# r times the decays: one multiply for a pair of heads, then DMAs into the zeroed tile

## The chip, the cores and the metric

The kernel runs on one core of a Trainium2 chip. The metric is the device time of one execution in microseconds (us); before the change the median of 3 runs is 726.37 us (724.88 to 728.85). A core has five engines, each with its own queue of instructions that it works off in order: TensorE (PE, with its weight loads as PEld), VectorE (DVE), ScalarE (ACT), GpSimd (POOL) and SyncE (SP, which here only issues DMAs). A DMA is issued by one of these queues and then moved by 16 shared DMA engines.

## The reference, cut to what matters

Three stages follow each other for 4 batches. Stage A is a linear recurrence over time for 8 heads of width 48, with a decay `w` per step and channel; stage B is a mixture of four causal attention experts; stage C is a feed-forward block. The change touches stage A alone:

```python
for t in range(S):                       # S = 768
    cur = np.einsum('bhd,bhe->bhde', u[None] * kt, vt)
    y[:, :, t] = np.einsum('bhd,bhde->bhe', rt, state + cur)
    state = wt[:, :, :, None] * state + np.einsum('bhd,bhe->bhde', kt, vt)
```

## The kernel before

**Stage A in chunks.** Time is cut into 6 chunks of 128 steps and heads are taken in pairs, so there are 16 pairs over the 4 batches. Head h of a pair stands in partitions 64h to 64h + 47. Within a chunk the products of decays come from two scans on DVE: `suf` (line 220, from the chunk's end) and `ex` (line 246, from its start). k is multiplied by `suf` into `kt` (line 234), r by `ex` into `rt` (line 255). Both multiplies read the transposed input straight from PSUM (`ptr`, line 201), three chunks (a half) at a time.

**Why `rt` is written per head.** `rt` has, for each chunk, 128 columns for head 0 and 128 for head 1. It is zeroed once (line 165), and head h's rows are written only into head h's columns, so that one matmul with `kt` (line 329, `pg`) gives both heads' 128x128 score blocks without mixing them. So line 255 runs four times per pair, for two halves and two heads, each on 48 partitions and 384 columns. There are two `rt` tiles, used in turn.

**From `rt` on.** `pg` is copied by ACT into `at` (line 337) and masked by POOL (line 338); `y_unit` sums `at` times v, and `rt` times the carried state `um`, in PSUM (`py`, line 368); ACT and DVE split the result into two parts (`xs`, lines 382 and 383), which a DMA stores. The state comes from `pu` (line 298) through DVE (`um`, lines 307 and 313). ACT overwrites `suf` and `ex` with their absolute values (lines 270 and 271) for a range check, once line 234 and line 255 have read them.

**What sets the order.** The program is written as generators that are interleaved: `a_prep` of the next pair is woven into `a_pair` of the current one, beside the streams of stage B and of `c_convert` (line 810), which turns the weights of stage C into pairs of tiles, one block after another (`c_raw` by DMA, then `c_w` on ACT and DVE, `c_hi`, `c_lo`). Batch 0 of stage A runs with nothing but weight loading beside it (about the first 75 us), the other three with stage B and the conversion beside it (to about 314 us). Then stage A's memory is released, the weights of stage C are loaded, and stages B and C share the rest. On top of this a scheduler places the instructions on each engine by its own estimate of their times, so a change of a few instructions moves others around them too.

**SP's queue.** In stage A nearly all DMAs are issued by SP in one order: the inputs of the next pairs (lines 180 and 195: `nw`, `nk`, `nr`, `nv`), `xs` (lines 404 and 412), `c_raw` and the stores of the conversion (lines 797 and 817), the second copy of k (line 571) and the input of stage B (line 529). A DMA that waits for an engine holds back those behind it.

Of the kernel before, what the change touches and what calls it, by code (L numbers as in the profile page):

```python
# [8 lines left out]
F32 = mybir.dt.float32  # L9
# [6 lines left out]
OP = mybir.AluOpType  # L16
# [7 lines left out]
C = 128  # L24
NC_ = S // C
# [87 lines left out]
def rwkv_moe_kernel(ctx, tc, r, k, v, w, u, wg, wq, wk, wv, wo, mu_k, mu_r, w_k, w_v, w_r, out):  # L113
    nc = tc.nc
# [9 lines left out]
    pA = stageA.enter_context(tc.tile_pool(name="pA", bufs=1, side="right"))  # L124
# [10 lines left out]
    def ps_a(nm):  # L135
        tag = cyc["tags"][cyc["n"] % len(cyc["tags"])]
        cyc["n"] += 1
        return (psA if tag == "a" else ps).tile([128, 512], F32, tag=tag, name=nm, bufs=PSB[tag])
# [47 lines left out]
    def a_load(p, nm):  # L186
        if p >= B * NP:
            return
        b, pr = divmod(p, NP)
        if nm[0] == "n":  # L190
            loaded[p, nm] = load_nat(SRC[nm], b, pr)
        else:
            loaded[p, nm] = nats[nm]
            for h in range(2):
                nc.sync.dma_start(nats[nm][:, :, h, 0:D], SRC[nm][b, 2 * pr + h].rearrange("(c p) d -> p c d", p=C))

    def tr_in(nat, f):

        pt = ps_a("ptr")
        for x in range(3):  # L200
            nc.tensor.transpose(pt[:, x * C : (x + 1) * C], nat[:, 3 * f + x].rearrange("p h d -> p (h d)"), ident)
        return pt[:, 0:HALF].rearrange("p (c x) -> p c x", x=C)
# [6 lines left out]
    def a_prep(b, pr):  # L209
        p = b * NP + pr  # L210
        nw, nk, nr, vn = (loaded.pop((p, x)) for x in ("w", "k", "r", "nv"))
        j = 2 * p
        halves = [slice(3 * f, 3 * f + 3) for f in range(2)]
        chunks = lambda t, x, o=0: t[:, o : o + NC_ * x].rearrange("p (c x) -> p c x", x=x)[:, :, 0:C]
        for f, cs in enumerate(halves):
            nc.scalar.copy(chunks(X, XC, 1)[:, cs], tr_in(nw, f))
        a_load(p + 1, "w")
        yield 1
        suf = pA.tile([128, XW], F32, tag="suf", name="suf", bufs=SUFB)
        nc.vector.tensor_tensor_scan(  # L220
            out=suf[:, ::-1], data0=X[:, ::-1], data1=d1[:, ::-1], initial=0.0, op0=OP.mult, op1=OP.add
        )
        yield 1
        kt = pA.tile([128, S], F32, tag="kt", name="kt", bufs=2)

        ku = pA.tile([128, NC_, 2, D], F32, tag="ku", name="ku", bufs=1)
        nc.gpsimd.tensor_tensor(
            out=ku, in0=nk[:, :, :, 0:D], in1=ub[:, None, 2 * pr : 2 * pr + 2].to_broadcast([128, NC_, 2, D]), op=OP.mult
        )
        rt = rts[p % 2]  # L230
        sh = bass.AP(tensor=suf.tensor, offset=suf[:, 2:3].offset, ap=[suf[:, 2:3].ap[0], [XC, NC_], [1, C]])
        for f, cs in enumerate(halves):
            pk = tr_in(nk, f)
            nc.vector.tensor_tensor(out=chunks(kt, C)[:, cs], in0=pk, in1=sh[:, cs], op=OP.mult)
        a_load(p + 1, "k")
        yield 1

        pc = pA.tile([128, NC_], F32, tag="pc", name="pc", bufs=2)
        pcs = suf[:, 1 : 1 + NC_ * XC : XC]
        nc.vector.reciprocal(out=F1[:, 0 : NC_ * XC : XC], in_=pcs)  # L240
        nc.scalar.copy(pc, pcs)
        pcx = pcxs[p % 2]
        nc.gpsimd.tensor_copy(pcx[:, :, 1:], pc[:, None, 2:NC_].to_broadcast([128, D, NC_ - 2]))
        yield 1
        ex = pA.tile([128, NC_ * XC], F32, tag="ex", name="ex", bufs=1)
        nc.vector.tensor_tensor_scan(  # L246
            out=ex, data0=X[:, 0 : NC_ * XC], data1=F1[:, 0 : NC_ * XC], initial=0.0, op0=OP.mult, op1=OP.add
        )
        yield 1
        ev = chunks(ex, XC)  # L250
        for f, cs in enumerate(halves):
            pr_ = tr_in(nr, f)
            for h in range(2):
                q = slice(64 * h, 64 * h + D)
                nc.vector.tensor_tensor(out=rt[q, cs, h], in0=pr_[q], in1=ev[q, cs], op=OP.mult)  # L255
        nc.vector.tensor_tensor(out=ku, in0=ku, in1=nr[:, :, :, 0:D], op=OP.mult)
        a_load(p + 1, "r")
        cc = pA.tile([128, NC_, 2], F32, tag="cc", name="cc", bufs=2)
        nc.vector.tensor_reduce(out=cc, in_=ku, axis=AX.X, op=OP.add)
        dg = dgt[p % 2]  # L260
        nc.gpsimd.tensor_tensor(
            out=dg[:, :, :, 0:D].rearrange("p c h d -> p h c d"),
            in0=vn.rearrange("p (h c) d -> p h c d", h=2),
            in1=cc.rearrange("p c h -> p h c")[:, :, :, None].to_broadcast([128, 2, NC_, D]),
            op=OP.mult,
        )
        dgs[b, pr] = dg
        kts[b, pr] = kt
        yield 1
        nc.scalar.activation(out=suf, in_=suf, func=AF.Abs, accum_out=chk[:, j : j + 1])  # L270
        nc.scalar.activation(out=ex, in_=ex, func=AF.Abs, accum_out=chk[:, j + 1 : j + 2])
        yield 1
        prep[b, pr] = (rt, kt, vn, pc)
        yield 1
# [147 lines left out]
    def phase_a(b):  # L422
        if b == 0:
            for _ in a_prep(0, 0):
                pass
            a_kt(0, 0)
            yield 5 * 109
        for pr in range(NP):
            nxt = (b, pr + 1) if pr + 1 < NP else (b + 1, 0)
            if nxt[0] < B:  # L430
                yield from weave(a_pair(b, pr, nxt), a_prep(*nxt), 7, 8)
            else:
                yield from a_pair(b, pr, None)
            a_load(b * NP + pr + 2, "nv")
# [7 lines left out]
        out=cmask, in_=cmask, pattern=[[-1, 128]], compare_op=OP.is_ge, fill=NEG, base=0, channel_multiplier=1  # L442
# [782 lines left out]
```

## Time and profile before

| What | Value |
|---|---|
| median of 3 runs | 726.37 us (724.88 to 728.85) |
| profiled execution, its own time | 727.12 us |
| its span (first to last instruction) | 725.4 us |
| PE busy | 672.8 us (93%) |
| DVE busy | 497.9 us (69%) |
| ACT busy | 409.2 us (56%) |
| POOL busy | 299.7 us (41%) |
| mean granted PE clock | 0.984 |

The span is divided below at 75 us and at 314 us, where the chain of waits shows the end of batch 0 and of stage A. A busy share is an average over such stages; the chain of waits follows the work that ended last back through the engines and says which of them a stage waited for. All of the change lies ahead of 314 us.

### The profile page before, as it was taken

The numbers are of one execution on the slowest core, as the hardware profiler recorded it, in microseconds if no ns is written. First come the engines' busy times: TensorE is split into PE (matmuls) and PEld (weight loads), VectorE is DVE, ScalarE is ACT, GpSimd is POOL, SyncE is SP. The second block draws the span as 40 slices with busy tenths as digits, with TensorE's granted clock in tenths as the row PEclk, the third lists the DMA queues.
The fourth block names the chain that finished last, engine by engine and source line by source line (L and its number), as shares of the span: only waits on it lengthen the run. The fifth ranks groups of instructions, "written<-read, shape, count | busy, mean of one in ns | idle before, by whom it ended". The sixth has DMA issues, their size and how long they took to land.

```text
span 725.4 us, 13681 instructions
## 1 busy us (share of the span) xinstructions
PE 672.8 (93%) x4938; PEld 585.4 (81%) x4938; DVE 497.9 (69%) x938; ACT 409.2 (56%) x1117; POOL 299.7 (41%) x397
## 2 busy tenths in 40 slices
PE   5887978889799999997999999999999999999995
PEld 4776856676577786866999899889898888989995
DVE  8988899998999888754543756556457573729520
ACT  3554556666576566656735657465556656534530
POOL 5876444343445222204625435362343515352320
PEclk9999899999999999999999999999999999999999
DMA  8797666668677653159320103211101101220001
GB/s 157 152 184 173 176 180 175 170 174 251 148 198 186 170 126 83 33 187 411 100 67 11 45 12 99 98 34 44 55 34 44 23 13 34 86 68 23 12 23 38
DMA packets 144205, 77.88 MB, mean 107 GB/s; under 512 B 109824, under 2 KB 138752, under 8 KB 143616
## 3 DMA queue, kind: packets, MB, share of 16 engines
q1 hardware_dynamic: 139936, 64.73, 35.1%
q0 software_dynamic: 864, 7.47, 2.6%
q10 hardware_dynamic: 3328, 4.72, 1.8%
q8 instruction: 41, 0.67, 0.4%
q14 instruction: 36, 0.29, 0.1%
HBM read 47.40 MB, written 23.99 MB: 98 GB/s over the span
## 4 chain that ended last, share of the span: by engine, by line
PE 64%; DVE 18%; DMA 8%; issue 4%; ACT 3%; POOL 1%; SPq 1%; ACTq 0%; DVEq 0%; POOLq 0%
PE ph L871 14%; PE pvo L871 14%; PE pz L871 5%; PE pa L710 5%; PE pq L518 4%; PE pt L681 3%; PE po L518 3%; PE py L368 3%; PE pv L518 3%; DMA c_raw<-in_moe_w_v_dram 2%; DVE ex L246 2%; PE psc L624 2%; PE pg L329 2%; DVE suf L220 2%; DVE rt L255 2%
## 5 line engine op out<-in xcount | busy, mean ns | idle before, releaser
L633 DVE TENSOR_REDUCE st<-psc 128x1 f32<-128x384 f32 (+4 forms) x128 | 62.1, 499 | 56.4 <-PE psc L629 41.3
L891 POOL TENSOR_TENSOR rl<-rl 128x256 f32<-128x256 f32 (+1 forms) x88 | 59.3, 678 | 78.5 <-ACT rl L890 78.3
L865 POOL TENSOR_TENSOR ml<-m,mh 128x256 fp32r<-128x256 f32 x54 | 40.6, 751 | 108.5 <-ACT mh L864 97.4
L645 ACT ACTIVATE A<-psc,st 128x384 f32<-128x384 f32 (+4 forms) x128 | 68.8, 542 | 20.2 <-DVE st L642 13.3
L871 PE MATMUL ph<-mh,ckh 128*128 128x256 f32 (+1 forms) x264 | 78.8, 299 | 0.9 <-ACT m L858 0.8
L871 PE MATMUL ph<-mh,ckl 128*128 128x256 f32 (+1 forms) x264 | 76.9, 292 | 1.5 <-DMA ckl<-ck_l_scratch 1.5
L338 POOL TENSOR_SCALAR_AFFINE_SELECT at<-at 128x512 f32<-128x512 f32 x48 | 44.7, 932 | 79.2 <-ACT at L337 79.0
L871 PE MATMUL ph<-ml,ckh 128*128 128x256 f32 (+1 forms) x264 | 76.9, 294 | 0.0
L871 PE MATMUL pvo<-cvh,hh 128*128 128x384 f32 x192 | 65.5, 341 | 0.0
L329 PE MATMUL pg<-rt,kt 128*128 128x256 f32 x192 | 53.8, 407 | 12.3 <-DVE um L307 5.8
L894 POOL TENSOR_TENSOR hl<-rl,hh 128x256 fp32r<-128x256 f32 x72 | 53.8, 756 | 27.0 <-ACT hh L892 26.7
L871 PE MATMUL pvo<-cvl,hh 128*128 128x384 f32 x192 | 64.6, 336 | 0.0
L871 PE MATMUL pvo<-cvh,hl 128*128 128x384 f32 x192 | 64.0, 336 | 0.0
L681 PE MATMUL pt<-ident,A 128*128 128x128 f32 x336 | 57.7, 275 | 0.0
L624 PE MATMUL psc<-k,q 128*128 128x384 f32 (+4 forms) x128 | 49.0, 383 | 9.0 <-ACT A L645 6.2
L890 ACT ACTIVATE rl<-ph 128x256 f32<-128x256 f32 (+1 forms) x88 | 35.5, 405 | 37.6 <-PE ph L871 26.2
L871 PEld LDWEIGHTS ph<-mh,ckh 128*128 128x128 f32 x264 | 49.9, 189 | 3.3 <-ACT m L858 1.0
L710 PE MATMUL pa<-at,vs 128*64 128x384 f32 (+2 forms) x288 | 52.1, 425 | 0.5 <-ACT at L694 0.5
L871 PEld LDWEIGHTS ph<-mh,ckl 128*128 128x128 f32 x264 | 50.0, 190 | 1.8 <-DMA ckl<-ck_l_scratch 1.8
L871 PEld LDWEIGHTS ph<-ml,ckh 128*128 128x128 f32 x264 | 49.9, 190 | 1.5 <-issue 1.5
L329 PEld LDWEIGHTS pg<-rt,kt 128*128 128x128 f32 x192 | 34.4, 197 | 19.8 <-DVE um L307 6.8
L861 DVE SCALAR_TENSOR_TENSOR m<-x2c,mu,m 128x256 f32<-128x256 f32 (+1 forms) x66 | 35.2, 539 | 20.4 <-ACT m L858 15.8
(172 smaller groups left out, 1917.3 us busy)
## 6 DMA issues: line engine op xcount, KB each, us to landing
x_scratch<-xs SPq DMA_DIRECT2D x24, 288.0 KB, 4.0
x<-x_scratch SPq DMA_DIRECT2D x6, 1152.0 KB, 8.4
nw<-in_w_dram SPq DMA_DIRECT2D x32, 144.0 KB, 3.7
nk<-in_k_dram SPq DMA_DIRECT2D x32, 144.0 KB, 3.1
nr<-in_r_dram SPq DMA_DIRECT2D x32, 144.0 KB, 2.8
nv<-in_v_dram SPq DMA_DIRECT2D x16, 288.0 KB, 3.2
out_dram<-rg SPq DMA_DIRECT2D x24, 192.0 KB, 1.9
c_raw<-in_moe_w_k_dram SPq DMA_DIRECT2D x12, 256.0 KB, 3.3
```

Source lines behind the costliest of these rows:

```text
L329: nc.tensor.matmul(pg[:, x * 2 * C : (x + 1) * 2 * C], lhsT=kt[:, c * C : (c + 1) * C], rhs=rt[:, c].rearrange("p h x -> p (h x)"), start= ...
L338: nc.gpsimd.affine_select(out=av, in_=av, pattern=[[0, 4], [1, C]], compare_op=OP.is_gt, fill=0.0, base=0, channel_multiplier=-1)
L518: nc.tensor.matmul(out, lhsT=a, rhs=c, start=i == 0, stop=i == n - 1)
L624: nc.tensor.matmul(o, lhsT=qs[e][:, tsl], rhs=ks[e][:, s0:s1], start=True, stop=False, skip_group_check=True)
L633: nc.vector.tensor_reduce(out=st[:, si : si + 1], in_=o, axis=AX.X, op=OP.max, negate=True)
L645: nc.scalar.activation(out=A[:, s0:s1], in_=p[:, 0 : s1 - s0], func=AF.Exp, bias=nm, accum_out=st[:, 3 + si : 4 + si])
L681: nc.tensor.transpose(pt[:, (j - j0) * 128 : (j - j0 + 1) * 128], A[:, j * 128 : (j + 1) * 128], ident)
L710: nc.tensor.matmul(pa[64 * e : 64 * e + 64, t0:HALF], lhsT=vs[:, j, 2 * pr + e], rhs=at[e][:, c0 : c0 + HALF - t0], start=j == 0, stop=j = ...
L865: eng.tensor_tensor(out=lo[:, j], in0=m1, in1=hi[:, j].bitcast(F32), op=OP.subtract)
L871: nc.tensor.matmul(out, lhsT=a, rhs=c, start=i == 0, stop=i == n - 1)
L891: nc.gpsimd.tensor_tensor(out=rl_, in0=rl_, in1=rl_, op=OP.mult)
L894: eng.tensor_tensor(out=hl[:, m], in0=rl_, in1=hh[:, m].bitcast(F32), op=OP.subtract)
```

## The change

For each half, DVE now multiplies all 128 partitions at once into a new plain tile `rp` (one buffer), in which the rows of both heads share the same columns. Then SP issues two DMAs for each half, one for each head, that copy 48 partitions x 3 chunks x 128 columns into that head's columns of `rt`. `rt` stays zero elsewhere as before. PE now waits for DMAs where it waited for DVE.

```diff
         ev = chunks(ex, XC)
+
+        rp = pA.tile([128, NC_, C], F32, tag="rp", name="rp", bufs=1)
         for f, cs in enumerate(halves):
             pr_ = tr_in(nr, f)
+            nc.vector.tensor_tensor(out=rp[:, cs], in0=pr_, in1=ev[:, cs], op=OP.mult)
             for h in range(2):
                 q = slice(64 * h, 64 * h + D)
-                nc.vector.tensor_tensor(out=rt[q, cs, h], in0=pr_[q], in1=ev[q, cs], op=OP.mult)
+                nc.sync.dma_start(rt[q, cs, h], rp[q, cs])
         nc.vector.tensor_tensor(out=ku, in0=ku, in1=nr[:, :, :, 0:D], op=OP.mult)
```

Per pair this is 2 instructions on DVE in place of 4, and 4 more DMAs in SP's queue; over 16 pairs 32 in place of 64, and 64 more DMAs. The scheduler's order moves with it, within stage A only: behind the last pair every engine's order is the same as before.

PE, batch 0, around the first `pg` of the third pair (`rt_86`; `ptr` with `nw` and `nk` are the transposes of the fourth pair's w and k). Before:

```order
49 L329 MATMUL pg<-rt_86,kt 128x256 x2
50 L298 MATMUL pu<-nv_82,kh 64x48 x5
51 L201 MATMUL ptr<-ident,nw 128x128 x3
52 L298 MATMUL pu<-nv_82,kh 64x48 x5
53 L201 MATMUL ptr<-ident,nk 128x128 x3
54 L329 MATMUL pg<-rt_86,kt 128x256 x3
```

And now:

```order
51 L201 MATMUL ptr<-ident,nw 128x128 x3
52 L201 MATMUL ptr<-ident,nk 128x128 x6
53 L349 MATMUL py<-ident,dg_84 128x128 x3
54 L332 MATMUL pg<-rt_86,kt 128x256 x2
55 L301 MATMUL pu<-nv_82,kh 64x48 x10
56 L332 MATMUL pg<-rt_86,kt 128x256 x4
```

The next pair's transposes and three of this pair's own transposes into `py` now stand ahead of the first `pg`, which used to stand ahead of them.

DVE at the same place (third pair: `ex`, the products with r, then `xs` and `um`, and `suf` of the fourth). Before:

```order
33 L246 SCALAR_TENSOR_TENSOR ex<-wx,d1f 128x774
34 L255 TENSOR_TENSOR rt_86<-ptr,ex 48x3x128 x4
35 L383 TENSOR_TENSOR xs<-py,xs 128x384 x2
36 L307 TENSOR_TENSOR um<-pu,pc 128x240
37 L220 SCALAR_TENSOR_TENSOR suf<-wx,d_77 128x775
```

And now:

```order
32 L246 SCALAR_TENSOR_TENSOR ex<-wx,d1f 128x774
33 L262 TENSOR_REDUCE cc<-ku 128x12
34 L316 SCALAR_TENSOR_TENSOR um<-pcx_91,um 128x240
35 L255 TENSOR_TENSOR rp<-ptr,ex 128x384 x2
36 L386 TENSOR_TENSOR xs<-py,xs 128x384 x2
37 L220 SCALAR_TENSOR_TENSOR suf<-wx,d_77 128x775
```

Two instructions stand where four stood, and the third pair's `um` now comes later, behind the next `suf`.

SP in the middle of stage A, at the tenth pair, where stage B's input (`x`, 1152 KB each) is loaded. Before:

```order
133 L529 DMA x<-x_scratch 128x6x384
134 L571 DMA k_1767<-k_1767 64x384
135 L529 DMA x<-x_scratch 128x6x384
136 L797 DMA c_raw<-in_moe_w_v_dram 128x384 x2
137 L817 DMA cv_h_scratch<-c_hi 128x192
138 L817 DMA cv_l_scratch<-c_lo 128x192
139 L195 DMA nr<-in_r_dram 128x6x48 x2
```

And now:

```order
142 L532 DMA x<-x_scratch 128x6x384 x2
143 L800 DMA c_raw<-in_moe_w_v_dram 128x384
144 L258 DMA rt_87<-rp 48x3x128 x4
145 L195 DMA nr<-in_r_dram 128x6x48 x2
146 L820 DMA cr_h_scratch<-c_hi 128x192
```

The four new DMAs of this pair stand directly behind the two large loads.

## Rows read from the trace of the kernel before

**Rows 1.** The page: busy time, share of the span, instructions.
```profile
span 725.4 us, 13681 instructions
PE 672.8 (93%) x4938; PEld 585.4 (81%) x4938; DVE 497.9 (69%) x938; ACT 409.2 (56%) x1117; POOL 299.7 (41%) x397
```

**Rows 2.** Busy time by stage: columns as named in the first line.
```profile
core 0: us, PE busy (x) PEld busy (x) DVE busy (x) ACT busy (x) POOL busy (x), PEclk, DMA share, GB/s
0.00:75.00 75.00, 59.08 (x505) 47.78 (x506) 65.30 (x90) 36.00 (x86) 54.18 (x68) 0.93 0.81 169
75.00:314.00 239.00, 215.04 (x1821) 173.57 (x1819) 209.88 (x428) 149.02 (x411) 89.95 (x101) 0.98 0.61 155
340.00:725.00 385.00, 377.63 (x2483) 349.44 (x2481) 208.77 (x389) 208.70 (x576) 149.86 (x218) 1.00 0.16 50
```

**Rows 3.** Chain of waits by line, shares: 0 to 75 us, then 75 to 314.
```profile
by line: issue 16.4%; PE pg L329 7.9%; DVE rt L255 7.2%; PE py L368 6.6%; DMA ub<-in_u_dram 6.2%; PE ptr L201 5.8%; SPq L195 4.7%; POOL wvl L461 3.5%; POOL ku L227 3.5%; DMA nr<-in_r_dram 3.5%; DVE suf L220 3.1%; DVE um L313 3.1%; POOL at L
...
by line: DMA c_raw<-in_moe_w_v_dram 7.2%; DVE ex L246 6.4%; PE py L368 6.2%; issue 5.7%; DVE suf L220 5.0%; DVE st L633 4.2%; PE pg L329 4.0%; DMA k<-k 3.8%; DVE c_w L805 3.7%; DVE rt L255 3.3%; DVE kt L234 3.2%; PE pq L518 2.8%; DMA c_raw<
```

**Rows 4.** Instruction groups to 320 us: busy us, mean ns, idle before, releaser.
```profile
L255 DVE TENSOR_TENSOR rt<-ptr,ex 48x384 f32<-48x384 f32 x64 | 35.4, 553 | 3.5 <-PE ptr L201 2.2
...
L234 DVE TENSOR_TENSOR kt<-ptr,suf 128x384 f32<-128x384 f32 x32 | 16.6, 539 | 0.1
...
L271 ACT ACTIVATE ex<-ex 128x774 f32<-128x774 f32 x16 | 13.6, 852 | 13.6 <-DVE rt L255 13.5
```

**Rows 5.** Chain of waits in batch 0 and after: start, us, what.
```profile
39.14 0.57 DVE rt L255
39.72 0.02 issue
39.74 0.48 ACT ex L271
...
47.85 2.60 DMA nr<-in_r_dram
...
85.14 3.60 DMA c_raw<-in_moe_w_k_dram
...
167.79 9.46 DMA c_raw<-in_moe_w_v_dram
...
218.48 2.52 DMA c_raw<-in_moe_w_v_dram
```

**Rows 6.** Timeline: rt and first pg of pairs 3, 6, 15 (start, us).
```profile
37.42 2.28 DVE L255 TENSOR_TENSOR rt<-ptr,ex 48x384 f32<-48x384 f32 x4
38.81 0.73 PEld L329 LDWEIGHTS pg<-rt,kt 128*128 128x128 f32 x4
...
77.97 1.12 DVE L255 TENSOR_TENSOR rt<-ptr,ex 48x384 f32<-48x384 f32 x2 [0.57 <-PE ptr L201]
87.67 0.36 PEld L329 LDWEIGHTS pg<-rt,kt 128*128 128x128 f32 x2
...
276.57 2.27 DVE L255 TENSOR_TENSOR rt<-ptr,ex 48x384 f32<-48x384 f32 x4
281.39 0.73 PEld L329 LDWEIGHTS pg<-rt,kt 128*128 128x128 f32 x4
```

**Rows 7.** DMA issues (count, KB, us to landing); then one line's issue durations, ns.
```profile
x<-x_scratch SPq DMA_DIRECT2D x6, 1152.0 KB, 8.4
k<-k SPq DMA_DIRECT2D x32, 96.0 KB, 2.1
x<-xs SPq DMA_DIRECT2D x6, 288.0 KB, 4.6
...
L571 SPq DMA_DIRECT2D k<-k x32: 461/482/571, 96.5 to 577.9; - x32
```

**Rows 8.** SP's own waits from 75 to 300 us: total, times, longest.
```profile
SPq L797 <- DVE c_w L805: 28.4, 17, 5.3
SPq L180 <- PE py L368: 27.9, 8, 4.7
```

**Rows 9.** SP's timeline in batch 0: start, us.
```profile
29.02 1.23 SPq L195 DMA_DIRECT2D nw<-in_w_dram  x2
30.35 1.43 SPq L412 DMA_DIRECT2D x<-xs  x2
...
36.14 2.83 SPq L195 DMA_DIRECT2D nr<-in_r_dram  x2
39.08 0.56 SPq L469 DMA_DIRECT2D st<-in_moe_wk_dram  x1
39.73 0.46 SPq L180 DMA_DIRECT2D nv<-in_v_dram  x1
```

## The prediction, made before the result was known

> **What bounds the kernel now.** I read the page first for its busy times, then busy time by stage, then the chain of waits by line, and the timeline around the instructions that change. The page alone misleads: PE is busy for 672.8 of 725.4 us and DVE for 497.9 [rows 1], as if DVE had much to spare. By stage it is otherwise: DVE is busy for 65.3 of the first 75 us and for 209.9 of the next 239 (87% and 88%), PE for 59.1 and 215.0 (79% and 90%) [rows 2]. From 340 us on PE is busy for 377.6 of 385 us and bounds alone, and nothing that stands there changes place. So the question is how much earlier stage A ends, and stage A is bound by no single engine: DVE and PE hand the chain to each other, with DMAs between them. The reader is to see in the chain's shares that line 255 holds 7.2% of the first 75 us, 5.4 us, and 3.3% of the next 239, 7.9 us [rows 3]. That is 13.3 us on the path of the 35.4 us that line 255 costs DVE [rows 4]; the other 22 us lie beside something later.
>
> **DVE's part.** 64 products of 48 partitions take 553 ns each, 35.4 us. The new form, 128 partitions x 384 columns from PSUM, is the form of line 234, whose 32 take 539 ns each [rows 4]. So 48 rows cost as much as 128, and 32 new products cost 32 x 0.539 = 17.2 us. DVE is relieved of 18.2 us. On the chain half of each term goes: 2.7 us ahead of 75 us, 3.9 us behind it, 6.6 us together. In an unchanged order that is the most to be had to first order, since the chain moves to another engine when one link shortens. What comes behind line 255 on the chain is mostly not `pg` but ACT, which may not overwrite `ex` before the product has read it [rows 5]; ACT waits 13.5 us in all for this [rows 4], and that wait ends 1.1 us earlier for a pair where DVE alone sets it. What is late next is `at`, `xs` and `wx` behind it on ACT, and PE.
>
> **The DMAs' part.** The trace has no DMA of this shape. Each moves 48 x 3 pieces of 512 bytes, 72 KB. The nearest row is the copy of k from one SBUF half to the other, 96 KB, which lands 2.1 us after its issue and holds SP for 482 ns; the DMA of `xs` into `x`, also from SBUF to SBUF, with four times the bytes, lands after 4.6 us [rows 7]. Nothing excludes more than either where the queue is full: a `c_raw` load behind the large `x` loads took 9.46 us [rows 5]. I take 2.1 us, the nearer row, and keep 4.6 for the range. The first `pg` needs both heads of the first half, so it waits for the second of two DMAs: 0.48 us for the first issue, then 2.1 us, 2.6 us behind the first product.
>
> How much of it is covered is read from the timeline, from the end of the second product (the first half's second head) to the first `pg`. Pair 3, in batch 0: the products end at 37.42 + 2 x 0.57 = 38.56, `pg` starts at 38.81, 0.25 us later. Pair 6: 77.97 + 1.12 = 79.09 to 87.67, 8.6 us. Pair 15: 276.57 + 1.14 = 277.71 to 281.39, 3.7 us [rows 6]. These are the extremes of pairs 6 to 16, eleven of them; the middle one has 5.4. The new first product ends 0.57 us before the old second one, so the first `pg` could start 2.6 - 0.57, about 2.0 us, behind the old mark. From pair 6 on 3.7 us or more cover this, with at least 1.7 us left over. In batch 0 only 0.25 us do, and about 1.8 us per pair would be exposed in pairs 3 to 5. There the new order places nine transposes of the next pair and three of its own ahead of the first `pg`, which is work that PE had to do anyway. I let it cover 1.1 of the 1.8 us (between none and all), so 0.7 x 3 = 2.1 us come back, and 0.3 us for the start of pair 1, which has no earlier pair to hide behind: 2.4 us (between 0 and 3 x 1.8 + 2.0 = 7.4).
>
> **SP's part.** 64 issues of 0.48 us are 31 us more in SP's queue, four for each pair: 20 of them ahead of 75 us, 44 behind it. From 29.0 to 40.2 us SP issues almost without a gap [rows 9], so in batch 0 about 2 us for each pair come out of little room. Behind 75 us there is room, but an issue in the wrong place delays what stands behind it: seven times between 85.14 and 218.48 us the chain runs through the landing of a `c_raw` load [rows 5], because ACT and DVE, which work in order, wait for it. If two new issues stand ahead of such a load in one case of eight or so, that is 7 x 0.12 x 1, about 0.8 us. It could be nothing, where the scheduler places them behind, or 7 x 1.9 = 13 us, where all four stand ahead each time. I take 0.8 us, since SP already holds issues of the same length between those loads.
>
> The Trainium skill bears on this term from the other side: its page "DMA: Bandwidth & Descriptors", section "Issuing engines are not separate DMA queues", says that the sequencer's time to start a DMA is usually small beside the DMA itself. By that rule this term would be zero and the sum 0.8 us lower; here the rows show 0.48 of 2.1 us, almost a quarter, in a queue that was nearly full in batch 0, so I do not follow it.
>
> **The sum.** The profiled execution took 727.12 us, 1.7 us more than its span. 727.1 - 6.6 + 2.4 + 0.8 = 723.7. The median of the runs shown, 726.37, lies 0.75 us below the profiled execution, so the forecast for the median is **723.0 us**. Its own range, with the order's own shifts of some 3 us either way, is 720 to 726.5.
>
> **Rivals.** *DVE was the bound all along.* For it: in 75 to 314 us DVE is idle for only 29 of 239 us, and the new order is free to fill what is gained. Then the whole relief behind batch 0 counts, 11 pairs x 4 x 0.553 - 11 pairs x 2 x 0.539 = 24.3 - 11.9 = 12.5 us less what PE cannot follow. PE has 24 us of idle time there [rows 2], which half of it may eat: 6 to 10 us, 716 to 720. Against it: line 255 is on the chain for only a third of its time.
>
> *The landing reaches PE (slower).* Place: the first `pg` of each pair from the sixth on, behind which PE's queue holds stage B. The first of the two DMAs is issued only when what stands ahead of it in SP's queue has got its own wait over, and SP waits for others often: `nv` loads 8 times and 27.9 us, up to 4.7 us, `c_raw` loads 17 times and 28.4 us [rows 8]. A wait of 1.7 us uses up what pair 15 has left, 3.4 us what the middle pair has; that is the point from which it decides. With a full 4.7 us in front, a pair of middle slack is late by 4.7 - 3.4 = 1.3 us and the tightest by 3.0, about 14 us over the eleven pairs; that is added to the forecast's sum: 723.0 + 14 = 737, and with half of it 730. For it: the four DMAs of the tenth pair stand directly behind two loads that take 8.4 us to land [rows 7]. Against it: the scheduler knows the wait and most slacks are long.
>
> *Batch 0 becomes bound by SP (slower).* If SP is full, four more issues of 0.48 us lengthen each of the four pairs behind the first by 1.9 us, 7.7 us, and a late `nr` load is on the chain already (2.6 us) [rows 5]. With no relief there and the 3.9 us behind it kept, 727.1 + 7.7 - 3.9 - 0.75 = 730.2. The Trainium skill would call this one of the ways to be DMA-bound, a sequencer's track solid with issues ("Perfetto Trace Analysis", section "What 'DMA-bound' means"). Against it: the stretch without gaps is 11 us long, not 75.
>
> *It is hidden anyway.* Each shortened link ends at another engine, the landings cost what is gained: 726 to 728.
>
> **How the numbers follow.** Forecast 0.40, DVE as the bound 0.25, landing 0.15, SP in batch 0 0.09, hidden 0.11. 0.5%, about what a measurement of this kernel can tell from no change, is 3.6 us: faster is below 722.7, slower above 730.0. The forecast lies at that edge: 0.18 of its 0.40 I count as faster, the rest as no change. Faster: 0.25 + 0.18 = 0.43. Slower: 0.15 + 0.09 = 0.24. No change: 0.22 + 0.11 = 0.33. The range leaves out the best part of the first rival and the worst of the landing case: 716.5 to 732.
>
> **What would show it.** Right: products with r at 0.54 us x 32; DVE's busy time down by 18 us, all ahead of 314 us; `pg` from pair 6 on without a wait for the new DMAs, which land in 2 to 3 us; the large weight loads at the end of stage A starting 3 to 4 us earlier; the stretch behind it as long as before. Wrong: PE waiting for the new DMAs by more than a few us in all, landings of 4 us or more as a rule, input loads in batch 0 coming later than the transposes want them, or the chain through `c_raw` growing.

## The result and the profile after

The changed kernel takes 735.68 us (median of 4 runs, 732.62 to 738.24), the kernel before 726.5 beside it; the ratio is 1.0122, 95% interval 1.0074 to 1.017. It is slower by 1.2%, where 723.0 us and a range up to 732 had been forecast. The profiled execution took 735.29 us.

The page's first lines answer to [rows 1]:

```profile
span 733.4 us, 13764 instructions
PE 676.8 (92%) x4938; PEld 590.5 (81%) x4938; DVE 473.2 (65%) x906; ACT 407.9 (56%) x1117; POOL 287.7 (39%) x397
```

DVE is busy for 24.7 us less, more than the 18.7 that line 255 gives (35.4 us before, 16.7 now); the span is 8.0 us longer. By stage, as in [rows 2]:

```profile
0.00:75.00 75.00, 55.49 (x491) 44.26 (x491) 53.80 (x75) 35.26 (x84) 48.37 (x65) 0.93 0.82 174
75.00:314.00 239.00, 214.42 (x1764) 174.60 (x1759) 192.96 (x404) 144.70 (x406) 83.02 (x102) 0.95 0.68 172
340.00:725.00 385.00, 382.38 (x2513) 353.88 (x2512) 212.55 (x396) 213.46 (x588) 151.50 (x221) 1.00 0.18 59
```

DVE went from 88% to 81% busy between 75 and 314 us, and PE got no further for it: with the same busy time (214.4 and 215.0 us) it did 1764 matmuls where it had done 1821, at a granted clock of 0.95 where it had 0.98. In the first 75 us PE did 491 instead of 505.

Three marks show where time is lost: the start of the sixth pair's `suf` on DVE (the first five pairs are done with it), the first `pg` of the seventh pair, and the first `ph`, the first matmul of stage C with the loaded weights. The first and the last of them in the timeline before:

```profile
69.01 2.29 DVE L220 TENSOR_TENSOR_SCAN suf<-wx,d 128x775 f32<-128x775 f32 x1
...
332.84 0.48 PE L871 MATMUL ph<-mh,ckh 128*128 128x256 f32 x2 [0.84 <-ACT m L858]
```

And after:

```profile
75.56 1.82 DVE L220 TENSOR_TENSOR_SCAN suf<-wx,d 128x775 f32<-128x775 f32 x1
...
340.95 0.48 PE L874 MATMUL ph<-mh,ckh 128*128 128x256 f32 x2 [0.24 <-issue]
```

From `ph` to the end it is 392.6 us before and 392.5 after: nothing changed there, and all of the 8.1 us arose ahead of it. 6.6 us had arisen by the sixth pair. By the seventh pair's first `pg` 0.6 us of that were left (112.8 and 113.4), and 7.5 us came behind it. The rows of the stretch from there to `ph`, before and then after (columns as in [rows 2]), say what these 7.5 us are:

```profile
112.79:332.84 220.05, 197.74 (x1662) 155.97 (x1660) 186.72 (x378) 137.24 (x384) 79.22 (x94) 0.99 0.63 165
113.44:340.95 227.51, 204.80 (x1664) 163.50 (x1663) 172.95 (x362) 137.48 (x389) 71.13 (x94) 0.95 0.66 175
```

PE did as many matmuls to within two and was idle for 22.3 us before and 22.7 after; it was busy for 7.1 us more, at a granted clock of 0.95 in place of 0.99. What was lost behind the seventh `pg` lies mostly in matmuls that took longer, and not in PE's waits.

The terms of the sum, in the groups to 330 us (busy, mean ns, idle before, releaser; compare [rows 4]):

```profile
L255 DVE TENSOR_TENSOR rp<-ptr,ex 128x384 f32<-128x384 f32 x32 | 16.7, 548 | 5.4 <-PE ptr L201 5.2
...
L274 ACT ACTIVATE ex<-ex 128x774 f32<-128x774 f32 x16 | 13.7, 853 | 9.2 <-DVE rp L255 9.1
...
L805 ACT ACTIVATE c_w<-c_raw 128x192 f32<-128x192 f32 (+1 forms) x34 | 13.5, 400 | 27.8 <-DMA c_raw<-in_moe_w_v_dram 12.4 <-DMA c_raw<-in_moe_w_k_dram 7.2 <-DMA c_raw<-in_moe_w_r_dram 7.1
```

The products cost what was forecast, 32 x 548 ns. ACT's wait for them fell from 13.5 to 9.1 us, but its wait for `c_raw` loads rose to 27.8 us from 12.0. The same line before:

```profile
L802 ACT ACTIVATE c_w<-c_raw 128x192 f32<-128x192 f32 (+1 forms) x34 | 13.7, 402 | 12.0 <-DMA c_raw<-in_moe_w_v_dram 6.9 <-DMA c_raw<-in_moe_w_k_dram 2.6 <-DMA c_raw<-in_moe_w_r_dram 1.9
```

The DMAs, as in [rows 7] (count, KB, us from issue to landing):

```profile
x<-x_scratch SPq DMA_DIRECT2D x6, 1152.0 KB, 8.9
...
rt<-rp SPq DMA_DIRECT2D x64, 72.0 KB, 2.3
```

The landing too is in the median what was forecast, 2.3 us (the longest of the 64 took 9.2). What was not is the way to it. Timeline of the third pair, in batch 0, where [rows 6] had 0.25 us from the products to `pg`:

```profile
38.88 1.98 SPq L195 DMA_DIRECT2D nr<-in_r_dram  x2
39.60 0.99 DVE L255 TENSOR_TENSOR rp<-ptr,ex 128x384 f32<-128x384 f32 x2
40.98 4.07 SPq L258 DMA_DIRECT2D rt<-rp  x4
45.91 0.89 PE L332 MATMUL pg<-rt,kt 128*128 128x256 f32 x3 [1.94 <-DMA rt<-rp]
```

The first product ends at about 40.1. SP is busy with two `nr` loads until 40.86; then four issues take 4.07 us in all, one of them 1.7, and the last one that `pg` waits for, the third of the four, lands at 45.77 (chain below): 5.8 us from the product to `pg` where 2.6 had been taken. So it is in each of the first five pairs: 4.8, 7.1, 5.8, 5.1 and 6.3 us. By the semaphores that `pg` waits for, the last DMA it needs is the second of the four issues in pairs 1 and 4 only; it is the third in pairs 3 and 5 and the fourth in pair 2, so DMAs of the other half stand ahead of it. The chain of waits of the first 75 us (start, us, what; shares of that stretch in its first line, as in [rows 3]):

```profile
by line: issue 10.5%; DMA rt<-rp 7.9%; DVE suf L220 7.5%; PE pg L332 7.3%; PE py L371 6.5%; DMA st<-in_moe_wq_dram 5.6%; DMA x<-xs 5.4%; POOL wvl L464 4.7%; ACT wx L216 3.8%; DVE kt L234 3.5%; DMA nw<-in_w_dram 3.4%; DMA st<-in_moe_w_gate_d
...
43.43 2.34 DMA rt<-rp
...
68.83 3.60 DMA rt<-rp
```

The DMAs now hold 7.9% of the chain, where line 255 had 7.2%: one link was replaced by another of the same weight. The waits of the first 75 us (us in total, times, longest):

```profile
PE pg L332 <- DMA rt<-rp: 6.4, 3, 2.7
...
PEld pg L332 <- DMA rt<-rp: 4.1, 2, 2.1
```

And SP's own waits from 75 to 330 us, to set beside [rows 8]:

```profile
SPq L258 <- DVE rp L255: 25.4, 4, 12.7
```

Behind 75 us no row names a wait of PE for the new DMAs, and yet there is one, at the tenth pair, whose copies stand behind the two large `x` loads (and one `c_raw` load between):

```profile
167.54 1.27 SPq L532 DMA_DIRECT2D x<-x_scratch  x2
...
171.04 2.67 SPq L258 DMA_DIRECT2D rt<-rp  x4
...
180.59 1.10 PE L332 MATMUL pg<-rt,kt 128*128 128x256 f32 x4 [1.44 <-ACT c_w L805]
```

The first two of these copies land at 180.22 and 180.45 us, 9.2 and 8.7 us after their issue. `pg` waits for both and starts 0.14 us behind the second; it does not read the `c_w` that the row names. PE was idle for 1.44 us there. SP stands still for the products behind 75 us, in four places and up to 12.7 us, with loads behind it.

### The profile page after: what moved, and what is told of

Read it like the earlier page. It is cut to its first block, busy times and chain, and to the rows that moved or that the text cites. A ratio compares the mean times of both kernels' runs of the same rounds, so it can differ in the third digit from the quotient of the medians.

```text
span 733.4 us, 13764 instructions
## 1 busy us (share of the span) xinstructions
PE 676.8 (92%) x4938; PEld 590.5 (81%) x4938; DVE 473.2 (65%) x906; ACT 407.9 (56%) x1117; POOL 287.7 (39%) x397
## 4 chain that ended last, share of the span: by engine, by line
PE 67%; DVE 13%; DMA 10%; issue 3%; ACT 3%; SPq 2%; POOL 2%; DVEq 0%; ACTq 0%; POOLq 0%
PE ph L874 14%; PE pvo L874 14%; PE pq L521 6%; PE pa L713 5%; PE pz L874 5%; PE pt L684 4%; PE py L371 3%; PE pg L332 3%; DVE suf L220 2%; PE po L521 2%; PE psc L627 2%; DMA c_raw<-in_moe_w_v_dram 2%; PE psc L628 2%; PE pv L521 2%; DMA ckl<-ck_l_scratch 1%
## 5 line engine op out<-in xcount | busy, mean ns | idle before, releaser
L894 POOL TENSOR_TENSOR rl<-rl 128x256 f32<-128x256 f32 (+1 forms) x88 | 58.9, 674 | 78.3 <-ACT rl L893 78.1
L648 ACT ACTIVATE A<-psc,st 128x384 f32<-128x384 f32 (+4 forms) x128 | 68.6, 541 | 20.2 <-DVE st L645 12.5
L332 PE MATMUL pg<-rt,kt 128*128 128x256 f32 x192 | 56.1, 423 | 19.2 <-ACT at L340 7.9
L341 POOL TENSOR_SCALAR_AFFINE_SELECT at<-at 128x512 f32<-128x512 f32 x48 | 38.1, 797 | 70.2 <-ACT at L340 61.3
L332 PEld LDWEIGHTS pg<-rt,kt 128*128 128x128 f32 x192 | 36.2, 206 | 27.9 <-ACT at L340 8.7
L893 ACT ACTIVATE rl<-ph 128x256 f32<-128x256 f32 (+1 forms) x88 | 35.4, 404 | 38.9 <-PE ph L874 27.7
```

Of the source, the lines that this page charges most:

```text
L332: nc.tensor.matmul(pg[:, x * 2 * C : (x + 1) * 2 * C], lhsT=kt[:, c * C : (c + 1) * C], rhs=rt[:, c].rearrange("p h x -> p (h x)"), start= ...
L341: nc.gpsimd.affine_select(out=av, in_=av, pattern=[[0, 4], [1, C]], compare_op=OP.is_gt, fill=0.0, base=0, channel_multiplier=-1)
L648: nc.scalar.activation(out=A[:, s0:s1], in_=p[:, 0 : s1 - s0], func=AF.Exp, bias=nm, accum_out=st[:, 3 + si : 4 + si])
L894: nc.gpsimd.tensor_tensor(out=rl_, in0=rl_, in1=rl_, op=OP.mult)
```

## The experiments

Ratios are to the kernel before on the same chip, with 95% intervals. The table gathers the three marks of each profile (us), the use that PE makes of copies in the first five pairs, and the ratio. The marks are of one execution of each kernel, and executions of one kernel differ too: e14's twelve lie between 721.94 and 729.7 us, and the one in its profile is the longest of them.

| kernel | PE reads copies, pairs 1 to 5 | sixth `suf` | seventh `pg` | first `ph` | ratio |
|---|---|---|---|---|---|
| before | no | 69.0 | 112.8 | 332.8 | 1 |
| after | yes | 75.6 | 113.4 | 341.0 | 1.0122 |
| e20 after, other order | yes | 76.3 | 114.4 | 336.4 | 1.0081 |
| e16 after, inputs earlier | yes | 72.7 | 114.5 | 341.5 | 1.0134 |
| e6 two DMAs a pair | yes | 78.3 | 120.0 | 340.2 | 1.0098 |
| e5 change in pairs 1 to 5 | yes | 76.6 | 115.9 | 336.9 | 1.0088 |
| e4 change in pairs 6 to 16 | no | 69.1 | 110.4 | 339.2 | 1.0121 |
| e2 relief alone | no | 67.8 | 107.2 | 329.9 | 1.0008 |
| e13 no products | no | 67.9 | 109.0 | 327.5 | 0.9958 |
| e15 relief, unread copies | no | 66.9 | 105.6 | 328.1 | 0.9977 |
| e19 the same, pairs 1 to 5 | no | 68.0 | 108.9 | 340.5 | 1.0102 |
| e18 the same, pairs 6 to 16 | no | 70.0 | 110.3 | 336.9 | 1.0056 |
| e1 before + unread copies | no | 69.2 | 112.1 | 349.3 | 1.0242 |
| e11 the same, small | no | 68.3 | 112.5 | 350.7 | 1.0205 |
| e10 the same, no wait | no | 67.0 | 109.1 | 336.7 | 1.0068 |
| e14 before, other order | no | 69.2 | 110.8 | 335.4 | 0.9997 |

### What VectorE's relief is worth

**e2_relief_alone** writes one product of 128 partitions straight into the first head's columns; there are no DMAs, and the heads are not separated, so the scores are not the reference's.

```diff
-            for h in range(2):
-                q = slice(64 * h, 64 * h + D)
-                nc.vector.tensor_tensor(out=rt[q, cs, h], in0=pr_[q], in1=ev[q, cs], op=OP.mult)
+            nc.vector.tensor_tensor(out=rt[:, cs, 0], in0=pr_, in1=ev[:, cs], op=OP.mult)
```

> VectorE's relief without DMAs: one product of all 128 partitions for each half is written straight into rt, into the columns of head 0, so the two heads are not kept apart and head 1's columns stay zero (that part of the computation is left out; matmuls and shapes are the same). 32 products of 0.54 us in place of 64 of 0.55 us, nothing added. Theories SP and landing: faster than before by 4 to 7 us, 719 to 722, since the relief itself is worth the 6.6 us of the chain or most of it. Theory order: no gain or a loss, 726 or more, if the order that the scheduler makes for the shorter products is itself the bad one.

726.97 us, 1.0008 (0.999 to 1.0026). The relief alone gives no gain that can be measured.

**e13_no_products** leaves the product with r out altogether (`rt` stays zero):

```diff
-                nc.vector.tensor_tensor(out=rt[q, cs, h], in0=pr_[q], in1=ev[q, cs], op=OP.mult)
```

> The kernel before without the products of r and the decays (rt stays zero; that part of the computation is left out): VectorE is relieved of all 35 us of line 255, twice what the change takes away, and no DMA is added. Theory of the prediction (line 255 is on the chain for 13.3 us, so its time is worth a third): 713 to 719. Theory cover (ScalarE, PE and the DMAs of stage A are as late as VectorE, so its relief is worth nothing, as the run with the relief alone suggests): 723 to 728.

722.78 us, 0.9958 (0.9929 to 0.9986): all 35.4 us of line 255 are worth 3 us. The waits to 315 us say why; first before, then without the products:

```profile
ACT ex L271 <- DVE rt L255: 13.5, 8, 2.8
```

```profile
ACT ex L268 <- DVE ex L246: 14.6, 12, 3.5
```

ACT's wait for DVE ahead of the absolute value of `ex` is as long without the product as with it. It now ends at the scan before. The instruction that ended a wait was not what made it long.

### What the DMAs cost without the relief

**e1_unread_dmas** leaves the four products as they are and adds the 64 DMAs, out of `rt` into a tile that nobody reads.

```diff
+        rp = pA.tile([128, NC_, C], F32, tag="rp", name="rp", bufs=1)
...
                 nc.vector.tensor_tensor(out=rt[q, cs, h], in0=pr_[q], in1=ev[q, cs], op=OP.mult)
+                nc.sync.dma_start(rp[q, cs], rt[q, cs, h])
```

> The kernel before (four products per pair on VectorE, straight into rt), with 64 DMAs added on SP's queue: behind each product the same 72 KB are copied from rt into a tile that nobody reads. No one waits for their landing, and VectorE is not relieved. Theory SP (the 64 issues of 0.59 us and the places they take in SP's queue hold back the loads of inputs and weight blocks behind them): slower by 6 to 10 us, 732 to 737, with ScalarE waiting for c_raw loads about as long as in the changed kernel (27 us to the end of stage A, against 11 before). Theory landing (it is the way rp, DMA, rt, pg that is too long for PE): 726 to 728, since no matmul waits for these DMAs. Theory order (the other order of the changed kernel costs the time, whatever moves the data): within 3 us of before.

744.08 us, 1.0242 (1.0221 to 1.0263): slower than the changed kernel, with no engine waiting for the copies. SP's own waits:

```profile
SPq L257 <- DVE rt L256: 34.8, 23, 13.9
```

SP stood for the products 23 times, with everything behind it. Two runs take that apart. **e10_no_wait** copies from a constant, so that SP waits for no product; **e11_small** keeps the waits and moves 48 x 16 bytes each:

```diff
+                nc.sync.dma_start(rp[q, cs], ident[q, None, :].to_broadcast([D, 3, C]))
```

```diff
+                nc.sync.dma_start(rp[q, 3 * f, 0:4], rt[q, 3 * f, h, 0:4])
```

> As the kernel before with 64 unread DMAs of the same shape on SP, but their source is a constant tile (the identity), so SP never waits for a product of VectorE ahead of them. Theory waiting (SP stands still at a DMA whose product isn't there yet, 17.9 us of such waits in the run with unread copies of rt, and the loads behind it come late): back to 726 to 731. Theory issuing (each of the 64 takes about 0.6 us and a place in SP's queue, waits or not): 738 to 746, as with the copies of rt.

> As the kernel before with 64 unread DMAs behind the same products and with the same waits, but each of 48 pieces of 16 bytes in place of 144 pieces of 512 (0.8 KB in place of 72 KB). Theory data (the 16 DMA engines are loaded to 0.7 in this stage, and 4.7 MB more make the loads slower): 726 to 730. Theories issuing and waiting: 738 to 745, less what a shorter issue gives back.

Without the wait 731.66 us, 1.0068 (1.0041 to 1.0095); with it and almost no bytes 741.94, 1.0205 (1.0181 to 1.023). By these differences (each kernel has an order of its own) about 5 of e1's 18 us go with issues and bytes and the rest with SP's waits; the bytes alone are worth 2 us. None of the three is late at the sixth pair (67.0 to 69.2): 20 more issues in batch 0 delay nothing there by themselves.

**e12_unread_act** lets ACT issue e1's copies, **e3_act_queue** the changed kernel's:

```diff
-                nc.sync.dma_start(rt[q, cs, h], rp[q, cs])
+                nc.scalar.dma_start(rt[q, cs, h], rp[q, cs])
```

> As the kernel before with the 64 unread copies of rt issued by ScalarE in place of SP: the same data and the same products waited for, SP's queue as before, and some 25 to 38 us more for ScalarE (56% busy). Theories of SP's queue (issuing or waiting): 726 to 732. Theory data: 738 to 746.

> The changed kernel with its 64 DMAs from rp into rt issued by ScalarE in place of SP. Theory SP's queue: what was lost behind batch 0 comes back, 726 to 731; the landing in batch 0 stays in (the early pairs alone cost 5.7 us). Theory landing in all batches: 734 to 738, no different from the changed kernel.

771.33 us (1.0608; 1.0585 to 1.0632) and 772.45 us (1.0635; 1.0597 to 1.0674). Most of that is no answer: from `ph` to the end takes 426 and 428 us where the others have 392, and the order of stages B and C changed as well, with 60 more matmuls behind `ph`. Only `ph` bears on the question, at 343.4 and 343.3, some 10.5 us later than before: nothing here makes ACT's queue a better place for the wait.

### The change without its landing, and in halves

**e15_relief_unread** has the changed kernel's two products and four DMAs for each pair, half by half, but the products go into the first head's columns of `rt` and the DMAs copy from there into a tile that nobody reads (the heads are not separated):

```diff
+            nc.vector.tensor_tensor(out=rt[:, cs, 0], in0=pr_, in1=ev[:, cs], op=OP.mult)
...
+                nc.sync.dma_start(rp[q, cs], rt[q, cs, 0])
```

> The run with the relief alone (one product of 128 partitions for each half, straight into rt's columns of head 0, heads not kept apart) with 64 unread DMAs of the changed kernel's shape behind the products on SP. Against the changed kernel only one thing is missing: no matmul waits for the landing. Theory waiting (SP stands still with loads behind it): 733 to 740, as slow as the changed kernel or slower. Theory landing: 726 to 729, as the relief alone.

724.07 us, 0.9977 (0.9963 to 0.9992): 64 DMAs at no cost. SP's waits for the products:

```profile
SPq L257 <- DVE rt L254: 10.2, 4, 4.9
```

Beside e1 (34.8 us in 23) SP stands still for much less here. The same products leave 25.4 us of it in the changed kernel and 24.6 in e18 below, so the order has its part in that. Against e1 the relief, worth nothing alone, is worth 20 us. And beside the changed kernel, whose only other difference is that PE reads the copies (and the order that the scheduler makes of it), 10 us seem to be the landing's. That reading was put to the test in halves. **e4_late_pairs** and **e5_early_pairs** make the change from the sixth pair on and in the first five alone; **e18_late_unread** and **e19_early_unread** are their twins with copies that nobody reads (heads not separated in those pairs):

```diff
+        rp = pA.tile([128, NC_, C], F32, tag="rp", name="rp", bufs=1) if p > NP else None
...
+                if rp is not None:
+                    nc.sync.dma_start(rt[q, cs, h], rp[q, cs])
```

> The change from the sixth pair on (44 DMAs); the first five pairs, those of batch 0 and the first of batch 1, as before. Theory landing, in the form of the prediction (only batch 0 lacks the slack): faster than before by 2 to 4 us, 722 to 724. Theory SP: slower by 5 to 9 us, 731 to 735, since in the changed kernel the pairs 10 to 16 lost 9 us against before (first matmul of the pair 16 at 311.1 against 303.2 us).

> The change in the first five pairs alone (20 DMAs), the eleven others as before. In the changed kernel the scan suf of pair 6 starts 6.6 us late, and by pair 8 the lag is 0.3 us. Theory landing in batch 0: slower by 4 to 7 us, 730 to 733, unless it is made up later. Theory SP in the later batches: 725 to 728, since the lag of batch 0 is made up by stage B's work, which fills the gaps behind it.

> The kernel before, with from the sixth pair on one product of 128 partitions written into the first head's columns (so the heads are not separated there) and 44 copies out of it that nobody reads; the first five pairs are as before. It has the relief, the issues and SyncE's standing still of the changed kernel's late pairs, and lacks only that TensorE reads what the copies bring. Theory 1, the landing in the late pairs costs the time that the change from the sixth pair on lost (734.4 us, ratio 1.0121): 723 to 727 us here. Theory 2, SyncE standing still before the product with loads behind it costs it: 731 to 735 us here too.

> The same for the first five pairs alone, 20 copies that nobody reads, the later pairs as before. Theory 1, the landing in the first five pairs costs what the change made there alone lost (731.59 us, ratio 1.0088): 724 to 727 us here. Theory 2, SyncE's issues and waits beside the first weights' loads cost it: 730 to 733 us.

Early: e5 731.59 us (1.0088; 1.0065 to 1.0112), its twin e19 735.61 (1.0102; 1.0067 to 1.0137). Late: e4 734.4 (1.0121; 1.0097 to 1.0145), its twin e18 730.96 (1.0056; 1.0034 to 1.0079). In e4 no row names a wait of PE for the copies.

The sixth pair's `suf`, in e5 and then in its twin, shows the landing in batch 0 by itself:

```profile
76.61 2.63 DVE L220 TENSOR_TENSOR_SCAN suf<-wx,d 128x775 f32<-128x775 f32 x1
```

```profile
67.99 1.76 DVE L220 TENSOR_TENSOR_SCAN suf<-wx,d 128x775 f32<-128x775 f32 x1
```

8.6 us, and the changed kernel against e15 gives 8.7 (75.6 and 66.9). In the table all five kernels in which PE reads copies there stand at 72.7 to 78.3 and the other eleven at 66.9 to 70.0. Of the kernels that are not in it, e3, in which PE reads copies, stands at 78.2, and e17 and e12, in which it reads none, at 70.8 and 71.9; only e9, whose `pg` has another form, is late without copies (79.1). This much is shown.

What becomes of it is not. e19 has no landing, is 8.6 us ahead at the sixth pair, and yet reaches `ph` 3.7 us after e5. From the seventh `pg` to `ph` both run the old code, and so do the kernel before and e14: 220.0 us in before, 221.0 in e5, 224.5 in e14 and 231.6 in e19, 11.6 us apart. Their orders there differ, and so do the executions that were profiled (e5's is the shortest of its six), so not all of this is the order's. e19 from 75 to 314 us, to set beside [rows 2]:

```profile
75.00:314.00 239.00, 209.26 (x1719) 170.94 (x1720) 208.12 (x427) 146.22 (x404) 84.56 (x101) 0.95 0.63 159
```

So the landing is there in batch 0, but neither theory accounts for the final times: e18, 730.96 us, stands at the lower edge of what theory 2 expected, and e19, 735.61, above what either did.

### The order alone

**e14_pace** and **e20_after_pace** change one cost in the planner's table, in the kernel before and in the changed one; about 980 and 2180 of some 9200 matmuls stand elsewhere in PE's order, and nothing is added or left out.

```diff
-    A_COST, B_COST, C_COST = 34000.0, 61000.0, 58000.0
+    A_COST, B_COST, C_COST = 34300.0, 61000.0, 58000.0
```

> The kernel before with one number of its planner changed, A_COST 34300 in place of 34000: no instruction is added or taken away, but about 980 of some 9200 matmuls and 270 of 2140 VectorE instructions stand elsewhere in stage A, nearly as many as the change moves (1170 and 290). It measures what a new order alone does. Theory order: 4 us or more away from before, to either side, so that differences of that size between the other runs mean little. Theories of SP's queue: within 2 us of before, 724 to 729.

> The changed kernel with the planner's cost of stage A set from 34000 to 34300, which puts about 2180 of 9198 matmuls elsewhere in TensorE's order and adds and removes nothing. Theory 1, the loss comes from the landing or from SyncE and so from what the change does under any order: 732 to 740 us. Theory 2, the order that the planner happened to make for the changed kernel is a bad one: 725 to 730 us.

e14: 726.53 us, 0.9997 (0.9974 to 1.0019). e20: 732.17 us, 1.0081 (1.0054 to 1.0108), just inside what the landing and SP theories expected. A part of the loss stays under another order. Its late stretch is 221.9 us, near the 220.0 of before, where the changed kernel has 227.5: in this execution that part is not there. But the six runs fall into two groups, 730.05 to 730.48 and 733.87 to 734.34 us, and the profile is of the lower; no row shows whether the upper one lacks it too.

### Other forms

**e6_two_dmas** sends one DMA for each head after both products, 32 in place of 64; **e16_inputs_early_after** gives the changed kernel two buffers for w and k, loaded a pair earlier, and **e17_inputs_early_before** does that in the kernel before; **e9_half_rows** needs neither zeros nor DMAs, with one matmul of 64 rows for each head.

```diff
+        for h in range(2):
+            q = slice(64 * h, 64 * h + D)
+            nc.sync.dma_start(rt[q, :, h], rp[q])
```

```diff
-        a_load(p + 1, "w")
+        a_load(p + 2, "w")
```

```diff
+                    nc.tensor.matmul(
+                        pgs[h][:, x * C : (x + 1) * C], lhsT=kt[q, c * C : (c + 1) * C], rhs=rt[q, c], start=True, stop=True
+                    )
```

> The changed kernel with two DMAs for each pair (one for each head, all six chunks, behind both products) in place of four: 32 issues, and SP stops once per pair in place of twice, but for the later product. Theory issuing: half of the loss comes back, 729 to 732. Theory waiting: no better than the changed kernel, 733 to 740, since SP stands still until the second product is there, and the first matmul waits for all six chunks.

> The changed kernel with two buffers for the inputs w and k, whose loads are issued a pair earlier, so that they are not late if SP stands still at a DMA of rt for up to 12.7 us. Theory late input loads: most of the loss comes back, 726 to 730. Theory landing: no change against the changed kernel, 733 to 738. If what is late behind SP's waits is c_raw, nothing comes back either; then ScalarE still waits some 27 us for c_raw.

> The kernel before with the same early loads of w and k, as the measure for the run above. All theories: 722 to 728, since in the kernel before engines wait only some 10 us in all for these loads (POOL 5.2 us for k, PE 4.5 us for w).

> VectorE's relief of the change with neither rt nor DMAs: PE multiplies 64 rows of the plain product tile for each head (kt and the product, state and the product), so the heads are kept apart by the rows and nothing has to be zeroed. 192 more matmuls of half the rows and columns, each pair of them into two PSUM banks, and ScalarE copies at in two pieces of 256 columns (48 more copies of about 0.4 us less what each is shorter, some 10 us in all). Theory SP's queue: the loss of the changed kernel is gone, 723 to 730, about as the relief alone. Rival: the pieces cost PE and ScalarE more than VectorE gains, 731 to 738.

e6: 733.56 us (1.0098; 1.0071 to 1.0125). Half the issues, but the first `pg` waits for both halves, and PE's waits for the copies grew to 12.5 us in 8. e16: 735.2 (1.0134; 1.0115 to 1.0153): earlier inputs do not lessen the loss. SP's waits for the products in e16:

```profile
SPq L259 <- DVE rp L256: 0.5, 1, 0.5
```

SP hardly stands still for the products here, nor in e6 (0.9 us) and e20 (3.0), where the changed kernel has 25.4 us of it; e16 is as slow all the same. So the changed kernel's loss does not need SP's standing still at the new DMAs. e17: 747.04 (1.0309; 1.0281 to 1.0338); `ph` is no later than before (332.0), the loss lies behind it, where the order changed too, so it says little. e9: 748.53 (1.03; 1.0262 to 1.0339). Its `pg` to 345 us:

```profile
L328 PE MATMUL pg<-rt,kt 64*128 64x128 f32 x384 | 50.2, 315 | 18.8 <-ACT at L333 10.6 <-DVE rt L252 3.5 <-DVE um L304 3.0
...
L333 ACT COPY at<-pg 128x256 f32<-128x256 f32 x96 | 32.7, 373 | 20.1 <-PE pg L328 20.0
```

A matmul of half the rows and half the columns took 315 ns, two of them 630, where the whole took 407 (before, the same stretch), and `pg` and ACT's copy, in twice as many pieces, wait for each other. No version that computes the reference was faster than the kernel before.

## Why the prediction was wrong, point by point

**VectorE's relief, 6.6 us on the chain: the term that failed first.** It was forecast as half of line 255's share of the chain. e2 measured it by itself as 0.6 us slower (0.7 faster to 1.9 slower by the interval), e13 the whole of line 255 as 3 us. A share of the chain is an upper bound, as the prediction said, but it was booked in full: ACT's 13.5 us behind the product turned into 14.6 behind `ex` in e13. Taking e2's zero in its place, the same sum gives 723.0 + 6.6 = 729.6 us, already no gain.

**The landing, 2.4 us: mis-sized.** By the sixth pair it is 8.6 to 8.7 us. The 2.1 us to land were right for the median (2.3); the last copy that `pg` needs took 2.3, 2.8, 2.3, 2.2 and 3.6 us in the first five pairs. "0.48 us for the first issue" was not right. The first DMA's issue starts behind the product by what SP is still issuing, 0.9 to 2.2 us in these pairs; issues take 0.6 us as a rule and up to 1.71, and in three of the five pairs two or three of them stand ahead of the one that `pg` waits for. From product to `pg` that makes 4.8 to 7.1 us, against 2.6, and the longest is pair 2, for which the sum has no term. [rows 9] showed SP without a gap at that place, but the prediction charged it to another term. The transposes placed ahead of `pg` did not hide all of it: after them PE still waited, 1.94 us in the third pair. That PE waits for no copy from the sixth pair on was right but for the tenth (1.44 us).

With e2's zero and 8.6 us in these two terms the sum would give 735.8, next to the 735.7 measured. That would be luck: the landing's delay is nearly made up by the seventh pair, and about as much is lost again behind it, in PE's busy time.

**SP's term, 0.8 us: too small, and in part open.** 20 more issues in batch 0 cost nothing there (e1, e10, e11, e19 at the sixth pair), so *batch 0 becomes bound by SP* fell. The Trainium skill says in "DMA: Bandwidth & Descriptors", section "Issuing engines are not separate DMA queues", that the time to start a DMA is usually small beside the DMA itself. Here it was a quarter (0.59 of 2.3 us), and still these four rows show no cost of it at the sixth pair. Over all of stage A, 64 copies without a wait cost 5 us (e10) and with waits 18 (e1), while with the relief they cost nothing (e15). The changed kernel's loss does not need SP's waits for the products, though: e16 has 0.5 us of them and loses as much. The chain through `c_raw` that was named as a sign grew as a wait, 12.0 to 27.8 us on ACT, though not as a share of the chain (7.2% and 6.5% from 75 to 314 us for the largest of those loads).

**The rivals.** *DVE was the bound all along* fell with e2 and e13. *The landing reaches PE* came near in time (737) and was wrong in place: it reaches PE ahead of the sixth pair, and behind it only at the tenth, the pair that the rival named. The mark that would have told it, the `pg` of batch 0, was in the sum at 0.7 us for each of three pairs.

**What stays open.** Of the 8.1 us at `ph`, 6.6 are there at the sixth pair: 8.7 of landing less some 2 us of relief (66.9 in e15 against 69.0). At the seventh `pg` they are nearly made up, and 7.5 arise behind it, 7.1 of them in PE's busy time and 0.4 in its idle time. For the cause of that part there are observations and no proof. The granted clock goes with it: half-clock stretches from the seventh `pg` to `ph` add up to 3.4 us in before and 20.5 in after. But e20 has 20.5 us of them there as well, and PE is busy for 197.7 us in it, as before. Up to `ph` they add up to 20.5 us in before, 34.1 in after, 13.7 in e15 and 42.9 in e1, and over the 18 profiles on SP's queue or without DMAs (the table's, e9 and e17) the correlation with the time of `ph` is 0.83; e2 has 30.7 us of them and is early. Kernels with the same code in that stretch differ by 11.6 us, in other orders and other executions, and executions of one kernel in one order by up to 9.0 us (e18, 724.85 to 733.83). What makes the clock fall more often in one of them than in another, and how much of the 7.1 us it is, no run here separates.

## What to carry to other kernels

An engine that is 87% busy and ends many waits can still be worth nothing: leave its work out once and see, before a relief is priced by its share of the chain. Price a DMA between two engines from the end of the producer to the start of the consumer, with what the issuing queue is doing at that moment and every issue ahead of the one that is waited for. And where a planner lays the order, take more than one order of a kernel and more than one execution of each before a per cent is put down to a cause: here equal code differed by 11.6 us in one stage.

## What the runs showed of the hardware that was not expected

The granted clock of PE falls from 2.4 to 1.2 GHz in short stretches, eight of them in the changed kernel up to `ph`, and each follows a slice in which PE was idle for about half of the time or more. Two places in the changed kernel (columns as in [rows 2]; PE busy first, PEclk third from the end):

```profile
119.00:122.40 3.40, 1.52 (x9) 1.04 (x7) 3.40 (x4) 1.38 (x4) 1.36 (x4) 1.00 0.92 259
122.40:125.80 3.40, 3.36 (x19) 2.22 (x19) 3.40 (x9) 2.06 (x6) 1.30 (x2) 0.50 0.89 205
187.30:190.70 3.40, 1.13 (x4) 0.68 (x4) 3.40 (x7) 1.30 (x5) 1.02 (x2) 0.99 0.95 219
190.70:197.50 6.80, 6.22 (x36) 4.99 (x36) 6.80 (x15) 4.07 (x10) 2.64 (x3) 0.50 0.19 45
197.50:201.00 3.50, 3.50 (x42) 2.84 (x41) 2.79 (x7) 3.13 (x12) 0.59 (x1) 1.00 0.63 142
```

In both places the half clock is there when PE has work again: 36 matmuls in 6.8 us at the lower level, then 42 in 3.5 us at the upper. The same four matmuls at either level, from the timeline:

```profile
193.00 0.64 PE L371 MATMUL py<-rt,um 128*48 128x128 f32 x4
...
199.30 0.39 PE L371 MATMUL py<-rt,um 128*48 128x128 f32 x4
```

So an idle PE was paid for a second time there. And DVE, the engine that was relieved, was busy for every microsecond of the first four of these slices. Its load comes in bursts, and only one of the four, the last, holds products of line 255 (two of them, at 195.74 us).

Fewer partitions did not make an instruction shorter: products of 48 partitions took 553 ns, products of 128 with the same columns 548.
